# Loading the first chunk of four batches as one group, four tokens to a partition, with the weights in separate tiles

## The chip, the cores and the metric

The kernel runs on one core of one Trainium2 chip. The metric is device time in microseconds (us): the median of repeated runs, each with the granted TensorE clock recorded (the share of full speed that TensorE was allowed, averaged over the run; in the traces of the two kernels it stands at 1.00 or at 0.50). A run counts as slow when it lies over 1.5% above the fastest of the same kernel; all comparisons here use fast runs. The profiled execution gives a span, from the first to the last instruction, which lies about 2 us below the time of the same run (193.5 and 195.28 us before, 201.2 and 203.32 after). Positions ("at 25.1") are microseconds from the start of the span.

Engines are named as the profile names them: PE (TensorE matmul), PEld (its weight loads), DVE (VectorE), ACT (ScalarE), POOL (GpSimd), SP (SyncE); a "q" behind a name is that engine's sequencer, which here mostly means the issuing of DMAs.

## The reference, cut to what matters

```python
batch, n_heads, seq, head_dim = 4, 8, 768, 48       # q, k, v, f_logit, float32
f = 1.0 / (1.0 + np.exp(-f_logit))
for t in range(S):                                   # a gated linear attention
    state = f[:, :, t, :, None] * state + np.einsum('bhd,bhe->bhde', k[:, :, t], v[:, :, t])
    y[:, :, t] = np.einsum('bhd,bhde->bhe', q[:, :, t], state)
x = y.transpose(0, 2, 1, 3).reshape(B * S, H * D)    # 3072 tokens x 384
h = x @ w_in                                         # 384 x 2048
out = (h * sigmoid(h)) @ w_out                       # 2048 x 384
```

The kernel cuts the 768 tokens into six chunks of 128. Within a chunk the recurrence becomes matrix products: sums of log f, keys and queries scaled by exponentials of these sums, masked scores, and a state that is carried from chunk to chunk. A *unit* is one chunk of one batch: units 0 to 3 are chunk 0 of the four batches. The two layers of the feed-forward part take most of TensorE's time. "First layer" below is `x @ w_in`; for chunk 0 it is 192 small matmuls, and nothing of the long, even part of the kernel can start before they are through.

## The kernel before

Every instruction is a task with an engine, a rank and the tiles that it takes and uses. A planner orders the tasks with an estimate of their durations; on the chip each engine then runs its own tasks in exactly that order. So an instruction that waits holds up everything behind it on its engine, needed or not: in the changed kernel GpSimd stood for 10.22 us at one cast, and two key products whose data were there stood behind it.

The loads put one token in each partition. One head of one token is 48 floats, so a piece is 192 bytes:

```python
def load(x, us):                                     # one DMA per tensor and unit, 192 KB
    ...
    nc.sync.dma_start(out=dst, in_=SRC[x].rearrange("b h s d -> s (b h) d")[c * C:(c + 1) * C, b * H:(b + n) * H])
```

Chunk 0 takes 16 such loads, in order of units: f, k, q, v of batch 0, then of batch 1, and so on. Batch 0 can be finished while batch 3 is still loading. v is used as it lands, after a cast on GpSimd (`vb`).

The weights w_in come in two halves and w_out in four pieces, issued by GpSimd as tasks of their own, each released by an earlier task. All halves are slices of one tile:

```python
w_in_sb = sb.tile([128, KT, d_ff], BF16, name="w_in_sb")
w_out_sb = sb.tile([128, NT, d_model], BF16, name="w_out_sb")
...
elif kind == "wi":                                   # half n of w_in
    nc.gpsimd.dma_start(out=w_in_sb[:, :, n:n + w], in_=w_in_src[:, :, n:n + w])
...
for kk in range(KT):                                 # first layer, one unit
    nc.tensor.matmul(h[:, r, :], w_tile(kk, 4 * j + r), at("xT", P)[:, kk, i * C:(i + 1) * C], ...)
```

While TensorE has nothing to do at the start, it runs matmuls on a blank tile ("blank" in the profile; 183 of them, 15.2 us, in the kernel before). They are meant for its clock; no run took them out, so their effect on it is not shown.

## Time and profile before

| what | value | how to read it |
|---|---|---|
| time | 193.28 us, median of 3 runs (192.56 to 193.48) | the metric |
| profiled span | 193.5 us, mean granted clock 0.981 | a run of 195.28 us, with a half clock for 6.8 us |
| PE busy | 179.7 us, 93% | the head holds most of the idle time |
| second half of w_in | issued 25.14, used from 34.16 | the chain of waits; 8.97 us |
| first layer of chunk 0 done | 45.2 us (40.52 + 4.69) | the last piece of that layer in the chain of waits (the work that ended last, followed back) |
| rest of the span | 148.3 us (193.5 - 45.2) | TensorE solid, then a tail of 3.6 us |

The prediction shows the lines. The number to keep is the last one. If the rest does not change, the whole effect of the change is where "first layer of chunk 0 done" moves to.

### The profile page before, as it was taken

The numbers are of one execution on the slowest core, as the hardware profiler recorded it, in microseconds if no ns is written. First come the engines' busy times: TensorE is split into PE (matmuls) and PEld (weight loads), VectorE is DVE, ScalarE is ACT, GpSimd is POOL, SyncE is SP. The second block draws the span as 40 slices with busy tenths as digits, with TensorE's granted clock in tenths as the row PEclk, the third lists the DMA queues.
The fourth block names the chain that finished last, engine by engine and source line by source line (L and its number), as shares of the span: only waits on it lengthen the run. The fifth ranks groups of instructions, "written<-read, shape, count | busy, mean of one in ns | idle before, by whom it ended". The sixth has DMA issues, their size and how long they took to land.

```text
span 193.5 us, 4915 instructions
## 1 busy us (share of the span) xinstructions
PE 179.7 (93%) x2027; PEld 144.8 (75%) x2027; DVE 92.5 (48%) x179; ACT 128.3 (66%) x214; POOL 69.7 (36%) x119
## 2 busy tenths in 40 slices
PE   5976873999999999999999999999999999999992
PEld 4966762997678978778878767878886786877851
DVE  4263556021689447679462776654315455622021
ACT  4425996379229699888897857797597685542700
POOL 2432457001449236173092568331317614200000
PEclk9999998599999999999999999999999999999999
DMA  6999999999999989998328659949994664512112
GB/s 126 202 185 190 223 178 206 205 200 217 205 242 253 232 181 240 194 223 204 72 54 169 152 118 207 200 91 175 184 204 108 152 157 95 136 24 61 41 44 81
DMA packets 119302, 31.12 MB, mean 161 GB/s; under 512 B 116288, under 2 KB 117184, under 8 KB 119280
## 3 DMA queue, kind: packets, MB, share of 16 engines
q1 hardware_dynamic: 116816, 24.32, 64.2%
q0 software_dynamic: 2464, 6.49, 13.8%
q8 instruction: 16, 0.26, 0.5%
q14 instruction: 6, 0.05, 0.1%
HBM read 25.17 MB, written 4.72 MB: 154 GB/s over the span
## 4 chain that ended last, share of the span: by engine, by line
PE 77%; DMA 9%; ACT 6%; SPq 3%; issue 2%; POOL 1%; DVE 0%; DVEq 0%; POOLq 0%
PE mlp L510 31%; PE mlp L500 27%; PE mlp L489 5%; DMA f<-in_f_logit_dram 5%; DMA w_in_sb<-in_moe_w_in_dram 5%; PE sc L553 3%; SPq L455 3%; ACT L631 3%; PE yd L566 2%; PE yd L562 2%; PE tq L542 2%; PE cs L519 2%; PE yd L584 2%; ACT ia L526 1%; PE tq L574 1%
## 5 line engine op out<-in xcount | busy, mean ns | idle before, releaser
L510 PE MATMUL mlp<-w_out_sb,hT 128*128 128x384 bf16 x384 | 69.9, 326 | 0.0
L496 ACT ACTIVATE hT<-mlp 128x512 bf16<-128x512 f32 x80 | 47.1, 597 | 22.4 <-PE mlp L500 19.6
L500 PE MATMUL mlp<-xT,w_in_sb 128*128 128x256 bf16 x480 | 58.3, 273 | 0.3 <-ACT hT L496 0.3
L500 PEld LDWEIGHTS <-w_in_sb 128*128 128x128 bf16 x480 | 51.0, 114 | 2.7 <-issue 0.4
L510 PEld LDWEIGHTS <-hT 128*128 128x128 bf16 x384 | 35.1, 97 | 19.4
L532 POOL TENSOR_TENSOR qk<-k,ia 128x384 bf16<-128x384 f32 x24 | 24.0, 998 | 50.0 <-ACT al L530 38.1
L557 DVE TENSOR_TENSOR atm<-sc,triu 128x512 bf16<-128x512 f32 x48 | 30.9, 685 | 15.4 <-PE sc L553 15.4
L631 ACT ACT_TABLE_LOAD x21 | 26.9, 1283 | 0.4
L595 POOL TENSOR_TENSOR st<-sd,al 48x192 bf16<-48x192 f32 x40 | 20.2, 504 | 13.0 <-DVE sd L589 8.5
L570 DVE CAST yb<-yd 128x384 bf16<-128x384 f32 x24 | 13.3, 555 | 23.7 <-PE yd L566 23.6
L513 DVE COPY o<-mlp 128x384 f32<-128x384 f32 x24 | 13.3, 555 | 22.3 <-PE mlp L510 22.2
L526 ACT ACTIVATE ia<-cs 128x384 f32<-128x384 f32 x24 | 11.7, 488 | 15.5 <-PE cs L523 11.7
L534 POOL CAST vb<-v 128x384 bf16<-128x384 f32 x24 | 11.7, 503 | 20.6 <-DMA v<-in_v_dram 11.1
L489 PE MATMUL mlp<-xT,w_in_sb 128*128 128x128 bf16 x192 | 14.3, 241 | 5.2 <-DMA w_in_sb<-in_moe_w_in_dram 5.0
L536 DVE TENSOR_TENSOR qk<-q,cs 128x384 bf16<-128x384 f32 x24 | 13.2, 549 | 10.0 <-ACT cs L528 9.9
L489 PEld LDWEIGHTS <-w_in_sb 128*128 128x128 bf16 x192 | 13.3, 121 | 5.6 <-DMA w_in_sb<-in_moe_w_in_dram 5.3
L606 PE MATMUL mlp<-blank 128*128 128x128 bf16 x183 | 15.2, 242 | 1.0 <-DVE blank L611 1.0
L462 ACT ACTIVATE e<-f 128x768 f32<-128x768 f32 (+1 forms) x14 | 10.4, 746 | 8.4 <-DMA f<-in_f_logit_dram 8.4
L544 DVE COPY qkT<-tq 128x1024 bf16<-128x1024 bf16 x13 | 8.9, 687 | 13.9 <-PE tq L542 13.9
L606 PEld LDWEIGHTS <-blank 128*128 128x128 bf16 x183 | 12.7, 110 | 1.4 <-DVE blank L611 1.0
L516 POOL DMA_DIRECT2D out_dram<-o x17 | 9.9, 580 | 10.4 <-DVE o L513 7.9
L486 ACT ACTIVATE hT<-mlp 128x512 bf16<-128x512 f32 x16 | 9.3, 597 | 6.0 <-PE mlp L489 5.5
(38 smaller groups left out, 147.1 us busy)
## 6 DMA issues: line engine op xcount, KB each, us to landing
f<-in_f_logit_dram SPq DMA_DIRECT2D x10, 384.0 KB, 6.1
k<-in_k_dram SPq DMA_DIRECT2D x10, 384.0 KB, 5.9
q<-in_q_dram SPq DMA_DIRECT2D x10, 384.0 KB, 5.5
v<-in_v_dram SPq DMA_DIRECT2D x10, 384.0 KB, 6.0
out_dram<-o POOLq DMA_DIRECT2D x17, 192.0 KB, 3.7
w_in_sb<-in_moe_w_in_dram POOLq DMA_DIRECT2D x2, 768.0 KB, 9.0
w_out_sb<-in_moe_w_out_dram POOLq DMA_DIRECT2D x4, 384.0 KB, 9.2
out_dram<-o SPq DMA_DIRECT2D x7, 192.0 KB, 1.9
```

The lines of the kernel that those rows point to most:

```text
L489: nc.tensor.matmul(h[:, r, :], w_tile(kk, 4 * j + r), at("xT", P)[:, kk, i * C:(i + 1) * C], start=(kk == 0), stop=(kk == KT - 1))
L496: return nc.scalar.activation(at("hT", P)[:, 2 * j:2 * j + 2, :], h, AF.Silu)
L500: nc.tensor.matmul(h[:, i, :], w_tile(kk, n), at("xT", P)[:, kk, :], start=(kk == 0), stop=(kk == KT - 1))
L510: nc.tensor.matmul(o, at("hT", P)[:, n, i * C:(i + 1) * C], w_out_sb[:, n, :], start=(n == 0), stop=(n == NT - 1))
L513: nc.vector.tensor_copy(at("ob", u), at("o", u)[:, 0:d_model])
L526: nc.scalar.activation(at("ia", u).rearrange("p h d -> p (h d)"), at("cs", u)[:, 0:HD], AF.Exp)
L532: nc.gpsimd.tensor_mul(at("qk", u)[:, 1, :, 0:D], at("k", P)[:, i], at("ia", u))
L557: nc.vector.tensor_mul(at("atm", u)[:, r], at("sc", u)[:, r], triu[:, None, :].to_broadcast([C, NP, C]))
L570: nc.vector.tensor_copy(at("yb", u), at("y", u))
L595: nc.gpsimd.tensor_mul(at("st", u)[lo:lo + D, :, r * D:(r + 1) * D], at("sd", u)[lo:lo + D, :, r * D:(r + 1) * D], at("al", u)[lo:lo + D, ...
L606: nc.tensor.matmul(buf["mlp", bank][:, 0:C], blank, blank, start=True, stop=True, skip_group_check=True)
L631: nc.scalar.preload_act_table_set(SETS[after[t.idx]])
```

## The change

The intent is to make the loads of chunk 0 cheaper and the vector work on them wider. The four batches' first chunks become one group: partition 32b + n holds tokens 4n to 4n + 3 of batch b. Four tokens of one head lie next to each other in memory, so a piece is 768 bytes instead of 192. The group has its own sums (`within`, `before`), mask (`quads`) and state products. v, which is needed with one token in each partition, is cast in the group's layout and then moved by small DMAs. Separately, the weight pieces get tiles of their own. The planner's ranks are new throughout. Cut to the core:

```diff
-    w_in_sb = sb.tile([128, KT, d_ff], BF16, name="w_in_sb")
-    w_out_sb = sb.tile([128, NT, d_model], BF16, name="w_out_sb")
+    w_in_sb = [sb.tile([128, KT, d_ff // NI], BF16, name=f"w_in{n}") for n in range(NI)]
+    w_out_sb = [sb.tile([128, NT // NO, d_model], BF16, name=f"w_out{n}") for n in range(NO)]
...
+        if kind in ("gf", "gk", "gq", "gv"):         # 8 loads per tensor, 96 KB each: half hh, batch b
+            hh, b = rest
+            src = SRC[kind[1]][b, 4 * hh:4 * hh + 4, 0:C].rearrange("h (n r) d -> n h (r d)", r=4)
+            to = at(kind[1], "g", hh)[32 * b:32 * b + 32]...
+            nc.sync.dma_start(out=to, in_=src)
...
+        elif kind == "gvb":                          # cast v, half hh, all batches
+            nc.gpsimd.tensor_copy(to, split(at("v", "g", hh)))
+        elif kind == "vp":                           # v of one batch to one token in each partition
+            lo = 32 * rest[0]
+            for r in range(4):
+                nc.sync.dma_start(out=at("vb", rest[0])[32 * r:32 * r + 32].rearrange("p h d -> p (h d)"),
+                                  in_=vb_group[lo:lo + 32, r].rearrange("p h d -> p (h d)"))
...
+            if not c:                                # x of chunk 0: tokens back in their order
+                x, t_ps = x.rearrange("p k (n r) -> p k r n", r=4), t_ps.rearrange("p k (r n) -> p k r n", r=4)
+            nc.vector.tensor_copy(x, t_ps)
```

The loads are issued in the order f, k, q of the first four heads, f, k, q of the other four, then all of v. GpSimd's order in the group is: first two key products, issue of w_in's first half, first v cast, last two key products, second v cast, two state updates, issue of w_in's second half.

## The prediction

> **What bounds the kernel now.** I read the page, then the chain of waits in order of time, the head of the timeline, and a table of stretches. From the page:
>
> ```profile
> span 193.5 us, 4915 instructions
> PE 179.7 (93%) x2027; PEld 144.8 (75%) x2027; DVE 92.5 (48%) x179; ACT 128.3 (66%) x214; POOL 69.7 (36%) x119
> ...
> PE   5976873999999999999999999999999999999992
> ...
> PEclk9999998599999999999999999999999999999999
> ```
>
> TensorE (PE) is solid from the eighth slice on and ragged before; the ragged part also holds 183 matmuls on a blank tile[...]. So there is a head of 34 us that waits, and a body that PE fills. The table of stretches (stretch, length, busy time of PE, PEld, DVE, ACT, POOL, granted clock, DMA share, GB/s) says the same:
>
> ```profile
> 25.10:34.20 9.10, 4.91 (x84) 4.00 (x81) 5.04 (x9) 6.90 (x12) 6.49 (x10) 0.91 1.03 188
> 34.20:47.00 12.80, 12.80 (x175) 12.22 (x176) 1.38 (x3) 8.30 (x13) 0.00 (x0) 0.80 1.05 203
> 47.00:70.00 23.00, 23.00 (x264) 17.43 (x262) 16.01 (x30) 14.27 (x26) 11.05 (x19) 1.00 1.06 224
> 70.00:110.00 40.00, 39.69 (x459) 32.15 (x457) 24.77 (x46) 35.00 (x61) 18.07 (x30) 1.00 0.84 173
> ```
>
> What ends the head stands in the chain (start, length, what) and in the timeline (with the idle time before and its releaser):
>
> ```profile
> 25.14 8.97 DMA w_in_sb<-in_moe_w_in_dram
> 34.16 4.03 PE mlp L489 x36
> ...
> 40.52 4.69 PE mlp L489 x84
> ```
>
> ```profile
> 25.14 0.82 POOL L475 DMA_DIRECT2D w_in_sb<-in_moe_w_in_dram  x1 [1.19 <-PE mlp L489]
> ```
>
> Only 48 of the 192 first-layer matmuls of chunk 0 run before the second half of w_in lands at 34.16. GpSimd (POOL) issued it at 25.14, after a wait of 1.19 us for matmuls that read the other half of the same tile. After it the matmuls take 4.03/36 = 112 ns, later 4.69/84 = 56 ns: some 2.5 us go to a half clock. They end at 45.2; the last matmul ends at 189.9 and the span at 193.5. So the end is "end of chunk 0's first layer" + 144.7 us of solid PE + 3.6 us of tail, and the change is read from the head.
>
> [...]after 3.03 us of PE idle the granted clock is 0.50 from 32.6 to 39.4. [...]the loads here are 192 B pieces, and in the first 8 us they arrive at 222 to 225 GB/s[...]. [...]while w_in's first half streams (9.9 to 14.3 us), some 88 packets of 192 B pass per us beside 91 of 2 KB; alone, over 1100 do. The 192 B loads nearly stop.[...]
>
> **The change part by part.** Chunk 0 of the four batches becomes one group: partition = batch and quarter row, four tokens in each, 768 B pieces, in two halves of four heads. The rest of the kernel is the same but for new ranks, one more transposed y by DMA (three PE transposes, 0.17 us, gone) and more stores from POOL.
>
> Loads. 16 loads of 192 KB become 32 of 96 KB on SyncE's queue. An issue with 128 pieces lasts 0.33 us here (the output stores) and 0.05 lies between issues: about 0.38 us each, 96 KB/0.38 = 259 GB/s at best, 12.2 us for all, where the old ones need 3.1 MB/0.22 = 14 us. An issue also waits for the landing of the eighth before it; with some 2.3 us to landing (2.9 for the first 192 KB) that just fits.
>
> Vector work. Exp and log go from 8 of 523 ns to 4 of about 840; the two exps of sums stay 8, the key and query products 4 + 4 at 1.0 and 0.55 us, the transposes 32, their copies 4. The 4 sums of 384 columns and 16 of one become 32 of 192 columns and 16 of four; the 16 state matmuls become 64 with a quarter of the rows. That is PE time in a head with 15.2 us of blank matmuls: free. The v cast stays near 2 us on POOL, and v must then be turned by 16 small SBUF-to-SBUF DMAs, which sit on SyncE's queue.
>
> The chain, walked with these durations: f of the first half lands at 4.2; exp and log to 6.0; sums at half clock, exps, first two key products on POOL to 10.4; w_in's first half issued at 10.4 (before: 6.9), data from 13.4 (3 us, as before). f of the second half waits for ScalarE, whose exps end at 13.9. POOL: v cast, key products 14.8 to 16.8, second v cast. The second v half is issued at 11.4 to 12.5, so part of it meets the w_in stream; with one 768 B packet per weight packet (16/0.21 = 77 per us, 59 KB/us) it lands at about 17.5. Cast to 18.5, state matmuls 1.8, state copies of batches 0 and 1, then their updates on POOL (1.05 each) to 23.2. There w_in's second half is issued: 1.9 us earlier than now. With the same 9.0 us it lands at 32.2.
>
> Scores, outputs and copies run on VectorE from 20.3, one batch per 2.2 us, so x of batch 0 is there at 28 and of the last at 31.5: the 48 matmuls of the first half of w_in fit before 32.2, and with them what the old kernel still did after 34.16 (y of batch 3 and its transposes, 0.5 us).
>
> Sum. First layer ends at 32.2 + 144 x 0.056 = 40.3, against 45.2: 2.0 from the earlier landing, 2.5 from the clock if PE stays awake, 0.5 from y. Then 144.5 + 3.6: 188.4. Against that: the weight stream now runs from about 26 to 37, and q and v of chunk 1, held behind the 16 v DMAs, are issued at 25 and starve until 37; at 220 GB/s they land at 39 to 42, while PE wants them at 40.5 to 44. w_out's last piece is issued only after a key product that needs ScalarE's exp after 16 silus, at about 44.5, and lands near 51.5; PE wants it at 50.5. I put 0.5 to 1 us of PE waits there. About 189.3.
>
> **Rivals.** (a) [...]If issues take 0.45 us[...], the second v half falls fully under the w_in stream, lands near 20 and moves everything after it: w_in at 34.5, end 190.5 to 192. For it: the v loads are last, and POOL takes its work in order.[...] (b) The opposite: issues of 0.33 us put all of v before the w_in stream; state updates end near 20.6, w_in lands at 29.6, end 186. (c) The half clock stays: between 13 and 28 us PE has small bursts and fewer blanks. Then the first layer takes 2.5 us longer: 191 with (a) absent. (d) Starvation after 40 us: q, v or w_out late by 3 us, end 191 to 192. (e) A gain in the body: none, it has no PE idle to give; the lower pace constant alone makes no matmul shorter.
>
> **Range and chances.** (a), (c) and (d) pull up by 1 to 3 us, (b) pulls down by 3; the landing of w_in, good to about 2 us, sets most of it. Range 186.2 to 192.2. The 2% line is 189.4, right at my number: faster 0.53, same 0.44, slower 0.03.
>
> **What would show it.** Right: second half of w_in issued near 23 and landed near 32; granted clock 1.00 from 28 on; first layer's end near 40; 144 us of solid PE after it. Wrong: w_in issued past 25; matmuls of 112 ns after it lands; PE idle between 40 and 55 released by q, v or w_out; or PE solid much earlier than 32, which would mean that the loads beat my 0.38 us.

## The result, and the profile after

The changed kernel is right, and slower: 203.36 us median of 4 runs (202.84 to 204.64), against 193.38 us (192.56 to 196.57) of the kernel before beside it. The ratio is 1.054, with a 95% interval of 1.047 to 1.061. Ratios here are the mean time of one kernel's fast runs over that of the other's in the same rounds, so they are not quite the ratio of the medians that stand beside them. All four runs of the changed kernel are of state fast; of the kernel before, 196.57 is slow.

The page of the profile after, its head:

```profile
span 201.2 us, 5007 instructions
...
PE   6790498589999999999999999999999999999992
...
PEclk9998557879999999999999999999999999999998
```

The digits are tenths of busy time in slices of 5.0 us. The fourth and fifth slice of PE, where it would have worked towards the first layer, are nearly empty (0 and 4), and from the fifth to the ninth slice the clock shows 0.5 to 0.8. From the tenth slice on PE is as solid as before.

The chain of waits tells where the first layer ends (start, length, what):

```profile
13.95 7.63 DMA v<-in_v_dram
...
29.72 1.48 SPq L593
...
33.15 4.99 DMA vb<-vb_group
...
44.44 8.04 PE mlp L636 x144
```

It ends at 44.44 + 8.04 = 52.5, which is 7.3 us later than in the profiled run of before, one of its slower runs. The rest of the span is 201.2 - 52.5 = 148.7 us, against 148.3. So the body is as it was, and the loss lies in the head. The chain names two things: a v load that takes 7.63 us to land, and the moves of v (line 593), of which one takes 4.99 us. Only the moves are new in kind. The chain of the kernel before has a slow load too, an f load of the third batch, under the same stream of w_in's first half:

```profile
7.28 9.25 DMA f<-in_f_logit_dram
```

And the last load of chunk 0 lands at the same time in both kernels, at 22.63 before and at 22.59 after (from the trace's landing events). What differs is how much waits for it: before, one batch; after, the whole group.

The timeline shows how they come about (start, length, engine, instruction, and in brackets the idle time before it and its releaser):

```profile
0.74 1.82 SPq L536 DMA_DIRECT2D f<-in_f_logit_dram  x4
...
10.59 0.93 POOL L622 DMA_DIRECT2D w_in<-in_moe_w_in_dram  x1
...
12.10 8.59 SPq L536 DMA_DIRECT2D v<-in_v_dram  x8
...
20.48 1.02 DVE L561 TENSOR_TENSOR hT<-q,mlp 128x384 bf16<-128x384 f32 x2 [7.18 <-DMA v<-in_v_dram]
...
21.74 0.82 POOL L589 CAST vb_group<-v 128x768 bf16<-128x768 f32 x1 [10.22 <-DMA v<-in_v_dram]
...
25.27 11.01 SPq L593 DMA_DIRECT2D vb<-vb_group  x16
...
30.42 0.82 POOL L622 DMA_DIRECT2D w_in<-in_moe_w_in_dram  x1
...
38.27 0.36 PE L713 MATMUL yd<-vb,atm 128*128 128x48 bf16 x8 [2.06 <-DMA vb<-vb_group]
```

Read it from the top. Four loads take 1.82 us and the next four begin at 2.60, so a load costs (2.60 - 0.74)/4 = 0.47 us of SyncE: 0.43 for the issue, 0.04 between two. The v loads, last in the order, therefore begin at 12.10, when the first half of w_in, issued at 10.59, is about to arrive. In the trace's packet records that stream starts at 12.3 and nearly all of it has started by 18.2. In the full microseconds from 13 to 18 only 24 to 87 packets of 768 B start; from 2 to 12 there were 240 to 307. So the last two q loads land at 17.6 and 20.4 and the v loads between 20.9 and 22.6. The prediction said that an issue also waits for the landing of the eighth DMA before it on SyncE's queue, and here that bites: the last two v loads are issued at 17.60 and 20.38, each 0.02 us after one of those q loads landed, and of SyncE's 8.59 us for the v loads 4.60 are this waiting. (VectorE's wait of 7.18 us for its second q product is put down to v by the profile; it reads q, whose last load landed at 20.36.) GpSimd stands for 10.22 us at the first v cast, and its last two key products, whose data were long there, stand behind it. Then SyncE is busy for 11.01 us with 16 moves of 24 KB each. A move lands 1.8 us after the start of its issue at first, and up to 6.1 us once the second half of w_in streams. The output products of the third batch wait for such a move until 38.27. GpSimd's issue of w_in's second half comes at 30.42, not at 25.14 as before.

The table of stretches (stretch, length, busy time of PE, PEld, DVE, ACT, POOL, granted clock, DMA share, GB/s) has the contrast in two rows:

```profile
2.00:12.00 10.00, 7.72 (x67) 7.35 (x65) 6.11 (x35) 4.74 (x9) 2.86 (x3) 1.00 0.76 203
13.00:20.00 7.00, 2.11 (x42) 1.93 (x39) 0.30 (x1) 1.76 (x5) 0.00 (x0) 0.91 1.06 214
```

In the first row the DMA engines are busy for 0.76 of the time: the loads do not fill them, SyncE's issues set the pace, at 203 GB/s. In the second they are full (a share of 1.06) and every compute engine is nearly idle, GpSimd wholly. From 52.5 on TensorE is solid: 144.22 busy of 144.50 us.

### The profile page after: what moved, and what is told of

It reads as the page before. It is cut to its first block, busy times and chain, and to the rows that moved or that the text cites. A ratio compares the mean times of both kernels' runs of the same rounds, so it can differ in the third digit from the quotient of the medians.

```text
span 201.2 us, 5007 instructions
## 1 busy us (share of the span) xinstructions
PE 182.4 (91%) x2035; PEld 146.6 (73%) x2035; DVE 97.9 (49%) x201; ACT 124.4 (62%) x205; POOL 72.4 (36%) x123
## 4 chain that ended last, share of the span: by engine, by line
PE 72%; SPq 10%; DMA 6%; ACT 4%; issue 3%; POOL 1%; DVE 1%; DVEq 0%; POOLq 0%; ACTq 0%
PE mlp L657 28%; PE mlp L647 25%; SPq L536 6%; PE mlp L636 6%; DMA v<-in_v_dram 4%; SPq L593 4%; PE sc L701 3%; DMA vb<-vb_group 2%; PE yd L713 2%; PE yd L709 2%; PE tq L689 2%; PE cs L666 1%; PE yd L733 1%; ACT L798 1%; ACT hT L643 1%
## 5 line engine op out<-in xcount | busy, mean ns | idle before, releaser
L657 PE MATMUL mlp<-w_out,hT 128*128 128x384 bf16 x384 | 70.2, 326 | 0.0
L647 PE MATMUL mlp<-xT,w_in 128*128 128x256 bf16 x480 | 58.6, 273 | 0.2
L647 PEld LDWEIGHTS <-w_in 128*128 128x128 bf16 x480 | 51.1, 114 | 2.9 <-issue 0.3
L679 POOL TENSOR_TENSOR qk<-k,ia 128x384 bf16<-128x384 f32 x20 | 20.0, 999 | 40.3 <-ACT al L677 29.8
L704 DVE TENSOR_TENSOR atm<-sc,triu 128x512 bf16<-128x512 f32 x40 | 25.7, 684 | 17.5 <-PE sc L701 17.5
L663 POOL DMA_DIRECT2D out_dram<-o x23 | 13.1, 568 | 29.1 <-DVE o L660 28.1
L660 DVE COPY o<-mlp 128x384 f32<-128x384 f32 x24 | 13.2, 555 | 20.9 <-PE mlp L657 20.8
L673 ACT ACTIVATE ia<-cs 128x384 f32<-128x384 f32 x20 | 9.8, 488 | 20.9 <-PE cs L670 16.5
L744 POOL TENSOR_TENSOR st<-sd,al 48x192 bf16<-48x192 f32 x32 | 16.1, 504 | 14.4 <-DVE sd L738 13.1
L681 POOL CAST vb<-v 128x384 bf16<-128x384 f32 x20 | 9.6, 505 | 18.7 <-DMA v<-in_v_dram 18.2
L522 ACT ACTIVATE e<-f 128x768 f32<-128x768 f32 x10 | 8.4, 836 | 9.7 <-DMA f<-in_f_logit_dram 9.7
L636 PE MATMUL mlp<-xT,w_in 128*128 128x128 bf16 x192 | 12.0, 226 | 0.0
L713 PE MATMUL yd<-vb,atm 128*128 128x48 bf16 x192 | 8.8, 184 | 3.5 <-DMA vb<-vb_group 2.1
L636 PEld LDWEIGHTS <-w_in 128*128 128x128 bf16 x192 | 11.6, 116 | 0.0
```

The source lines that it names most:

```text
L647: nc.tensor.matmul(h[:, i, :], w_tile(kk, n), at("xT", P)[:, kk, :], start=(kk == 0), stop=(kk == KT - 1))
L657: nc.tensor.matmul(o, at("hT", P)[:, n, i * C:(i + 1) * C], w_rows(n), start=(n == 0), stop=(n == NT - 1))
L660: nc.vector.tensor_copy(at("ob", u), at("o", u)[:, 0:d_model])
L663: (nc.sync if t.eng == "SP" else nc.gpsimd).dma_start(out=out[r0:r0 + C, :], in_=at("ob", u))
L679: nc.gpsimd.tensor_mul(at("qk", u)[:, 1, :, 0:D], at("k", P)[:, i], at("ia", u))
L704: nc.vector.tensor_mul(at("atm", u)[:, r], at("sc", u)[:, r], (triu if c else quads)[:, None, :].to_broadcast([C, NP, C]))
```

## The experiments

The theory after this reading: two costs of about 4 us each. First, the last q loads and the v loads, issued at 0.47 us each, fall under the stream of w_in's first half, and GpSimd's order carries the delay to all else. Second, the 16 moves of v cost SyncE 11 us and land late under the second half's stream. The rivals: one of the two hides the other; the moves are harmless and only late v matters; the 32-partition loads are slow at the memory itself; or the group's form is slower whatever the loads do.

The table gives the times and the span's split for all runs. "Rest" is the span less the end of chunk 0's first layer; the layer's end is the start of its last piece in the chain plus that piece's length. Medians are of all runs, ratios of the fast ones; every profiled run but that of batch_order (one look, state unknown) is fast. In tiles_w_sooner the chain doesn't pass through the layer's last piece, so its two places are empty. The labels that end in _b repeat an experiment whose edit had a flaw, told below.

| kernel | median us (runs) | ratio to before, 95% | span | first layer ends | rest |
|---|---|---|---|---|---|
| before | 193.38 (192.56 to 196.57) | | 193.5 | 45.2 | 148.3 |
| after | 203.36 (202.84 to 204.64) | 1.054 (1.047 to 1.061) | 201.2 | 52.5 | 148.7 |
| w_after_v | 199.55 (199.23 to 199.97) | 1.041 (1.036 to 1.047) | 197.2 | 48.5 | 148.7 |
| moves_split | 200.85 (200.48 to 201.37) | 1.048 (1.043 to 1.052) | 199.4 | 50.8 | 148.6 |
| moves_split_b | 200.41 (199.65 to 201.76) | 1.037 (1.029 to 1.045) | 197.6 | 48.9 | 148.7 |
| v_from_pool | 199.05 (198.82 to 199.96) | 1.039 (1.034 to 1.044) | 197.5 | 48.8 | 148.7 |
| one_move (wrong result) | 199.31 (198.85 to 199.89) | 1.033 (1.028 to 1.037) | 197.4 | 49.0 | 148.4 |
| w_after_v_one_move (wrong result) | 194.96 (194.47 to 197.0) | 1.012 (1.006 to 1.018) | 192.6 | 44.1 | 148.5 |
| one_move_w_sooner (wrong result) | 195.0 (194.09 to 196.09) | 1.011 (1.004 to 1.018) | 193.6 | 45.2 | 148.4 |
| one_move_w_sooner_b (wrong result) | 194.67 (193.43 to 195.3) | 1.010 (1.007 to 1.013) | 193.1 | 44.7 | 148.4 |
| w_after_v_moves_split | 201.53 (200.13 to 201.78) | 1.043 (1.035 to 1.051) | 199.4 | 50.8 | 148.6 |
| w_after_v_moves_split_b | 201.45 (201.18 to 202.09) | 1.041 (1.035 to 1.046) | 199.2 | 50.6 | 148.6 |
| batch_order | 202.93 (1 run) | | 200.9 | 51.7 | 149.2 |
| tiles_only | 189.67 (189.39 to 192.02) | 0.988 (0.984 to 0.991) | 188.3 | 40.0 | 148.3 |
| tiles_w_sooner | 191.72 (191.1 to 192.32) | 0.994 (0.991 to 0.997) | 189.3 | | |
| tiles_w_sooner_b | 191.02 (190.13 to 191.16) | 0.985 (0.980 to 0.991) | 189.1 | 40.8 | 148.3 |

The last column hardly moves. Whatever an edit did, it did to the head. The kernel before varies more from run to run (191.07 to 194.74 in one set of 19, with granted clocks of 0.982 to 1.000), and its profiled run (195.28 us) is one of the slower ones: beside that set's fastest it would count as slow. Differences among the changed kernels are therefore better read from their own medians and spans than from the ratios.

A flaw of four edits was found only in their traces. The planner places the blank matmuls by the planned start of the task that comes next. A task that I moved *forward* kept its late planned start, and so all blanks up to that start came with it, in one heap in front of useful matmuls: 37 of them, 4.15 us, in moves_split, 10 in the changed kernel at the same place. In the _b runs the moved task takes the start of its new neighbour, and the blanks stay where they were. w_after_v moves a task backward and has no such heap; nor have one_move, w_after_v_one_move, v_from_pool, batch_order and tiles_only.

### w_after_v: the first weight stream behind the v loads

GpSimd issues w_in's first half after the second v cast. Nothing else changes; `behind` moves one task in the planned order.

```diff
     tasks, idles = planned(CFG, SLOTS)
+    behind(("wi", 0), ("gvb", 1))
```

> The changed kernel with one move: GpSimd issues the first half of w_in behind the second v cast instead of before the first one. Theory 1 (starvation: the w_in stream of 13.0 to 18.5 us holds up the last v and q loads, GpSimd waits 10.2 us for v and everything after it slides): the v loads are then bound by their issue alone (32 issues of 0.47 us), the first v cast starts near 16 us instead of 21.7, the second ends near 20 instead of 25.2, the second half of w_in is issued near 25 instead of 30.4, and the first layer ends 4 to 6 us earlier than at 52.5: about 198 us against 203.4. Theory 2 (the cost is SyncE's issue queue: 32 loads and 16 v moves, one after the other): little changes before 18 us and the v moves still take 10 us: 201 to 203. Theory 3 (the head's extra TensorE and VectorE work and its half clock cost the time): no change, 203.

Measured: 199.55 us, 3.8 us less than the changed kernel. The timeline of this run:

```profile
12.10 4.75 SPq L543 DMA_DIRECT2D v<-in_v_dram  x8
...
16.91 0.82 POOL L596 CAST vb_group<-v 128x768 bf16<-128x768 f32 x1 [7.20 <-DMA v<-in_v_dram]
...
20.43 11.78 SPq L600 DMA_DIRECT2D vb<-vb_group  x16
```

The eight v loads start at the same 12.10, but are through in 4.75 us instead of 8.59, and the first cast runs at 16.91 instead of 21.74. So the stream did hold the v loads, by 4.8 us. It held the last q loads as well: VectorE's second q product runs at 14.28 here, against 20.48. So the 3.8 us belong to the last loads together. The moves now begin at 20.43 and meet the delayed first half of w_in: they take 11.78 us of SyncE. The first cost is shown; the second stays.

### moves_split and moves_split_b: the moves from two engines

The moves are issued directly behind the second v cast, and every other one by ScalarE. The second run has the blanks in their old places.

```diff
+    behind(("vp", 0), ("gvb", 1))                    # and vp 1, 2, 3 behind it
...
-                nc.sync.dma_start(out=at("vb", rest[0])[32 * r:32 * r + 32]...
+                (nc.scalar if r % 2 else nc.sync).dma_start(out=at("vb", rest[0])[32 * r:32 * r + 32]...
```

> The changed kernel with the 16 v moves issued half by SyncE and half by ScalarE (idle then), all directly behind the second v cast. Theory 2 (issue queue): the moves take 5 us from 25.3 instead of 11.0, most of them pass before the second w_in stream starts at 32, the last y is not held to 42.0 by a move, and the first layer ends 3 to 5 us earlier: about 199 us. Theory 1 alone (only the v loads matter): the second half of w_in still lands at 39, so at most the part after 39 is saved, under 2 us if the moves were not what held y: 201.5 to 203.

> moves_split repeated without a flaw of its edit: there the tasks moved forward in the order kept their late planned start, and 37 blank matmuls (4.15 us), which are placed by that start, came in one heap before the last transposes of chunk 0 instead of 10 there and 27 later. Here the blanks stay where they are in the changed kernel. If the heap was what ate the gain, TensorE's transposes come at about 25 again and the time falls from 200.85 to 198 to 199. If ScalarE's eight issues are what ate it (its exponential of chunk 1 at 30 again, second half of w_in late), it stays at 200 to 201.

Measured: 200.85 us with the heap of blanks, 200.41 without; a gain of about 3 us, at the lower end of what was expected first, and less than the 198 to 199 that the repetition would have shown if the heap had eaten the gain; it fell in the other branch, 200 to 201, in which ScalarE's eight issues did. The timeline of moves_split_b:

```profile
24.72 7.89 SPq L604 DMA_DIRECT2D vb<-vb_group  x8
24.72 6.00 ACTq L604 DMA_DIRECT2D vb<-vb_group  x8
...
30.76 0.84 ACT L533 ACTIVATE e<-f 128x768 f32<-128x768 f32 x1 [16.05 <-DMA vb<-vb_group]
```

The moves are issued in 7.89 us beside 6.00, where 16 from one engine took 11.01. Of the 16, 13 are issued before w_in's second half, at 29.86. ScalarE pays: its exponential of the next chunk, which ran at 24.80 in the changed kernel, comes at 30.76. The second issuing engine saves some 3 us of issuing (7.89 against 11.01), and the time falls by some 3 us (200.41 against 203.36).

### v_from_pool: the v loads from GpSimd, at the start

```diff
-            nc.sync.dma_start(out=to, in_=src)
+            (nc.gpsimd if kind == "gv" else nc.sync).dma_start(out=to, in_=src)
...
+        early = [t for t in tasks if t.name[0] == "gv"]     # emitted before anything else on GpSimd
```

> The changed kernel with the 8 v loads issued by GpSimd, which is idle from 1.8 to 8.4 us, at its start instead of last on SyncE's queue. Theory 1: v lands before 10 us, GpSimd has no wait of 10 us, the second key products follow ScalarE at 14 to 16, the second v cast ends near 17, the second half of w_in is issued near 22 and lands near 31, the v moves run from 17 to 27, and the first layer ends near 40 to 42: 191 to 194 us. Theory 2: the moves on SyncE still take 10 us but start 8 us earlier, so nearly the same number; it differs from theory 1 only in what holds y. Theory 3: 201 to 203.

Measured: 199.05 us, 4.3 us less than the changed kernel, but 5 us or more above the 191 to 194 expected. The timeline shows who suffers instead:

```profile
11.90 0.83 POOL L589 CAST vb_group<-v 128x768 bf16<-128x768 f32 x1
12.09 1.02 DVE L561 TENSOR_TENSOR hT<-q,mlp 128x384 bf16<-128x384 f32 x2 [5.45 <-DMA q<-in_q_dram]
...
19.80 1.94 POOL L561 TENSOR_TENSOR hT<-k,ia 128x384 bf16<-128x384 f32 x2 [7.07 <-DMA k<-in_k_dram]
```

The first v cast no longer waits, but the loads of k and q do. From 4 to 12 us the DMA engines are now full (a share of 0.98 to 1.12, at 220 to 251 GB/s): with two engines issuing, the DMAs are the bound. The last k and q loads are issued between 9.8 and 14.8 and fall under the stream of w_in, issued at 11.09. So the delay is not v's alone. It goes to whichever loads come last, and all 3.1 MB need 12.5 to 14.3 us at that rate. This corrected the theory: the first cost is "a weight stream started before the last load", not "v too late".

### one_move: four moves instead of sixteen, wrong result on purpose

One DMA of 128 partitions per batch, with the same 96 KB, that puts tokens in the wrong partitions.

```diff
-            lo = 32 * rest[0]
-            for r in range(4):
-                nc.sync.dma_start(out=at("vb", rest[0])[32 * r:32 * r + 32].rearrange("p h d -> p (h d)"),
-                                  in_=vb_group[lo:lo + 32, r].rearrange("p h d -> p (h d)"))
+            nc.sync.dma_start(out=at("vb", rest[0]).rearrange("p h d -> p (h d)"),
+                              in_=vb_group[:, rest[0]].rearrange("p h d -> p (h d)"))
```

> Wrong result on purpose: the changed kernel with 4 moves of v, one of 128 partitions for each batch, in place of 16 of 32 partitions (the rows land in a wrong order; all counts and waits of the other engines stay). If the 16 moves hold the head's end (each issue 0.63 us on SyncE, the last ones caught by the second w_in stream, the last y held to 42.0 us), the moves end near 27.5, the second half of w_in lands at 39 as before, the 144 first-layer matmuls start at 39 to 40 instead of 44.4, and the time falls by 4 to 5 us, to about 199. If they are covered by other waits: 202.5 to 203.5.

Measured: 199.31 us, 4.1 us less than the changed kernel. The same bytes move, from the same tile to the same tiles; only the number of DMAs and the span of partitions of each differ. The timeline has the four moves:

```profile
24.95 2.48 SPq L591 DMA_DIRECT2D vb<-vb_group  x4
```

SyncE spends 2.48 us in place of 11.01, and all moves are issued before w_in's second half, at 30.10. Issue time is per DMA here: 2.48/4 = 0.62 us for 128 partitions, where 32 partitions took 0.59 and 0.04 between two. So four DMAs of 24 KB cost four issues where one of 96 KB costs one, and in this pair of runs the difference is worth 4.1 us of the time.

### w_after_v_one_move: both, wrong result on purpose

Both edits above together.

> Wrong result on purpose: the same 4 moves, and the first half of w_in issued behind the second v cast (w_after_v, 199.6 us). If the two are separate costs that add, the second half of w_in lands near 35 and nothing else holds the first layer: it starts dense at 35 to 36 instead of 40.3, and the time is about 195, still over the 193.2 of before; what then remains is the group's own chain (loads at the same rate as before, one group's sums, state and scores before any first-layer work). If the moves cost nothing here: 199.5.

Measured: 194.96 us, 8.4 us less than the changed kernel. Alone the two gave 3.8 and 4.1, together 7.9. So neither hides the other, and together they carry the kernel from 203.4 to within 1.2% of the kernel before. The chain's last piece of the first layer:

```profile
36.08 8.04 PE mlp L641 x144
```

The layer ends at 44.1, 8.4 us sooner than after. That is also 1.1 sooner than in the profiled run of before, which is one of its slower runs (195.28 us). In time this kernel is still 1.2% slower.

### one_move_w_sooner and one_move_w_sooner_b: the second weight stream earlier still, wrong result on purpose

With both costs gone the group kernel is still not faster than before. These runs ask whether the landing of w_in's second half is what is left. It is issued directly behind the first half; the first run also had a heap of 20 blanks.

```diff
     behind(("wi", 0), ("gvb", 1))
+    behind(("wi", 1), ("wi", 0))
```

> WRONG RESULT ON PURPOSE, as in w_after_v_one_move (195.0 us), from which only the issue of the second half of w_in differs: directly behind that of the first half (20.5 us) instead of behind two state updates (25.75). Question: what makes up the remaining 5.3 us over the before kernel with separate weight tiles (189.7)? Theory 'landing': the second half lands at 34.7 there and sets the start of the 144 dense matmuls at 35.9; with all of w_in landed near 32 the end comes 2 to 3 us sooner, 192 to 193. Rival 'order': VectorE's y copies, scores masks and x copies (busy without a gap from 28.5 to 35.7 us) set that start, and the end moves by less than 1 us; if the earlier stream delays the moves or f of chunk 1, it becomes worse (196).

> WRONG RESULT ON PURPOSE. one_move_w_sooner repeated without its heap of 20 blank matmuls, which held the state products by about 1.4 us. If VectorE's order is the bound of what is left: the start of the dense matmuls as in w_after_v_one_move (36.1) and 194.5 to 195. If the landing of w_in is: 192 to 193.

Measured: 195.0 and 194.67 us, against 194.96 without the edit. In the second run the second half was issued at 21.82 instead of 25.75, and yet the 144 dense matmuls began no earlier:

```profile
20.90 1.71 POOL L629 DMA_DIRECT2D w_in<-in_moe_w_in_dram  x2
...
36.47 8.20 PE L643 MATMUL mlp<-xT,w_in 128*128 128x128 bf16 x144
```

The edit moved the landing far less than the issue. By the trace's landing events the second half landed at 34.48 instead of 35.31, after 12.66 us instead of 9.56, with the first half in flight beside it (both issued from 20.90). It also pushed the landing of the last two moves from 30.0 and 30.2 to 31.5 and 33.2. So these runs test an issue 3.9 us sooner, not a landing 4 us sooner. What they do show is that here the landing does not end last: the dense matmuls begin 2.0 us after it (0.6 us after it without the edit).

What is left can be read in the chain of w_after_v_one_move:

```profile
19.50 1.07 PE mlp L760 x10
...
26.59 1.38 PE mlp L760 x14
...
28.46 0.56 DVE yb L722
```

and in its stretches (columns as above):

```profile
25.00:37.20 12.20, 11.02 (x190) 9.88 (x189) 10.59 (x17) 5.12 (x9) 6.16 (x11) 0.89 1.11 214
```

From 18.9 to 28.5 the chain runs through TensorE: transposes, the group's state products (twice 1.39 us) and, between them, four heaps of blanks (line 760), 3.74 us in all. From 28.5 to 34.2 it runs through VectorE, which is busy for 10.59 of the 12.20 us of the stretch with the masks, casts and x copies of all four batches, one after the other. In the kernel before, three of the four batches had passed through VectorE by 31 us, because batch 0 started on its masks at 10.30. In the group nothing of that can start before the last load. That the order on TensorE and then VectorE's queue are what is left is read from the chain and this row; no edit here shows it, and no run took the blanks out.

### w_after_v_moves_split and w_after_v_moves_split_b: both repairs that keep the result right

```diff
+    behind(("wi", 0), ("gvb", 1))
+    behind(("vp", 0), ("gvb", 1))                    # and vp 1, 2, 3 behind it; every other move from ScalarE
```

> Right result: the changed kernel with both repairs that keep it right: first half of w_in issued behind the second v cast, and the 16 moves of v issued directly behind that cast, half by SyncE and half by ScalarE. Theory 1 (two costs, v held under the weight stream and 16 moves issued one by one): the costs add, but half of the moves' cost stays: 203.4 - 3.8 - 2.5 = about 197. Rival: ScalarE's eight issues again delay its exp and with it GpSimd's second w_in issue, and nothing is gained over w_after_v alone: 199 to 200.

> w_after_v_moves_split repeated without the heap of 37 blank matmuls. If the costs add and half of the moves' cost stays: 197 to 198. If the moves under the first weight stream and ScalarE's issues cancel the gain: 199.5 or more, as w_after_v alone (199.55).

Measured: 201.53 us, and 201.45 without the heap of blanks. The costs do not add here; the two repairs together are 1.9 us worse than w_after_v alone (199.55), and above both branches that the first run expected (197, or 199 to 200). The timeline of the second run:

```profile
20.41 12.66 SPq L605 DMA_DIRECT2D vb<-vb_group  x8
...
28.39 0.84 ACT L534 ACTIVATE e<-f 128x768 f32<-128x768 f32 x1 [13.58 <-DMA vb<-vb_group]
```

Eight moves now take SyncE 12.66 us, longer than sixteen did in w_after_v (11.78) and than eight in moves_split_b (7.89). From moves_split_b this run differs only in the issue of w_in's first half, which comes at 20.33, with the moves: they are in flight while it streams, and one of them takes 7.71 us to land in the chain. ScalarE's exponential is late again (28.39). The two repairs work against each other: delaying the stream puts it on top of the moves.

### batch_order: neighbouring loads on other partitions

The batches are loaded in the order 0, 2, 1, 3, so that consecutive loads write different halves of the 128 partitions.

```diff
-        for b in range(BATCHES):
+        for b in (0, 2, 1, 3):
```

> The changed kernel with the group's loads issued in the batch order 0, 2, 1, 3 instead of 0, 1, 2, 3, so that neighbouring loads write different halves of the partitions.[...] the number of packets in a microsecond stays at 250 to 280 if SyncE's issue of 0.47 us is the bound[...].[...] The time stays within 1 us of 203.4 either way.

Measured in one look: 202.93 us, and about the same rate (195 GB/s from 2 to 12 us, against 203 in the changed kernel). A packet of 768 B took 45 ns in the mean from 2 to 12 us, and 36 ns in the median, in this run as in the changed kernel. From 2 to 11 us, 223 to 282 packets start in a microsecond, against 240 to 307, and the DMA share is 0.79. The order of the batches makes no difference at this rate, at which SyncE's issues set the pace. Whether it would at a higher rate, no run shows.

### tiles_only: the kernel before, with separate weight tiles alone

```diff
-    w_in_sb = sb.tile([128, KT, d_ff], BF16, name="w_in_sb")
+    w_in_sb = [sb.tile([128, KT, d_ff // NI], BF16, name=f"w_in{n}") for n in range(NI)]
...                                                    # likewise w_out, and the two places that read them
```

> The kernel before with one part of the change alone: w_in and w_out in separate tiles, nothing else. If the whole-tile wait of the prediction is real (GpSimd waited 1.19 us for first-layer matmuls before it issued the second half, and first-layer matmuls of the first half were held to its landing), the second half is issued at 24 instead of 25.1, matmuls on the first half go on while it is under way, and the time falls by 1 to 2 us: about 191.5 against 193.2. If these waits were covered by others: no change, within 0.5 us.

Measured: 189.67 us, ratio 0.988 (0.984 to 0.991). It is within 2%, but the whole interval lies below 1: it is faster than both kernels. The chain of waits:

```profile
23.92 7.43 DMA w_in<-in_moe_w_in_dram
31.40 2.20 PE mlp L494 x36
```

GpSimd issues the second half at 23.92 instead of 25.14: the wait of 1.19 us for matmuls that read the other half is gone. It also lands in 7.43 us instead of 8.97; why that is so, no run shows. The data are used from 31.40, 2.8 us sooner, and the 36 matmuls take 2.20/36 = 61 ns each instead of 112: TensorE stood idle for 0.26 us before them and not 3.03, and the granted clock is 1.00. In runs of before with a clock near 1.00 the time is 191.1 to 192.2. So about 2 us of the gain are there without the clock, and the rest goes with it.

### tiles_w_sooner and tiles_w_sooner_b: and the second half sooner still

```diff
+    behind(("wi", 1), ("vb", 2))                      # on top of tiles_only: issued at 19.11, in _b at 18.67
```

> A try for a better kernel: the kernel before with the weights in separate tiles (tiles_only, 189.7 us) and the second half of w_in issued one key product sooner, behind the third v cast (about 19.8 us instead of 23.9; batch 3's loads have then been issued). It lands near 29 instead of 31.3, the first layer starts there, and the time falls by 1 to 2 us to about 188. If the stream catches batch 3's loads, its x comes later than 35.4 and the gain is lost: 189.5 to 191.

> tiles_w_sooner repeated without its heap of 28 blank matmuls. If the loss of 2 us against tiles_only came from the stream that meets the loads of batch 3: 191 to 192 again. If it came from the heap: 189 to 190, or less if the earlier landing pays.

Measured: 191.72 us with a heap of 28 blanks, 191.02 without (runs of the clock 1.00: 190.13 and 190.92, against 189.41 to 190.35 of tiles_only). No gain, and by its own times about a microsecond of loss; the ratios to before (0.985 and 0.988) do not separate the two. So part of the first loss may have been the heap. The timeline of the second run shows why 5 us of earlier issue bring nothing:

```profile
20.25 7.21 SPq L468 DMA_DIRECT2D k<-in_k_dram  x1
```

and its chain has the load that matters:

```profile
19.11 10.00 DMA f<-in_f_logit_dram
```

The stream meets the loads behind it. An issue of chunk 1's k holds SyncE for 7.21 us, and the v cast of batch 3 on GpSimd waits 4.37 us, to 27.79, where tiles_only has it at 24.79. In the chain it is chunk 1's f, which lands after 10.00 us, at 29.1. ScalarE's exponentials of chunk 1 wait for it, and the activations of chunk 0's first layer stand behind them until 33.78. The second half of w_in had landed at 27.49, 3.9 us sooner than in tiles_only, and bought nothing. It is the lesson of v_from_pool once more: a stream that is started before the last load is paid for by that load.

## Why the prediction was wrong

The prediction was 189.3 us in a range of 186.2 to 192.2. The time is 203.36, so even the range failed, and the direction too. The sum has a slip as well: it adds positions in the span and gives the result as the time, which lies about 2 us higher; 189.3 us of span would be some 191 us of time. That is small beside a miss of 14 us.

**What held.** The frame held: the end is "end of chunk 0's first layer" plus a constant. The constant was 148.3 and measured 148.7. There was no gain in the body (rival (e)), and the half to one microsecond of PE waits after 40 us did not come. The first half of w_in was issued at 10.59 (predicted 10.4). The second half of w_in took 7.4 us from issue to landing (predicted 9.0), the first 10.0. The two gains named for the separate tiles and the clock are real, but they belong to the tiles alone: tiles_only has them.

**The step that failed first: "about 0.38 us each, 96 KB/0.38 = 259 GB/s".** I took the 0.33 us of output stores. An issue of these loads measured 0.43 with 0.04 between two. At 96 KB in 0.47 to 0.48 us the new loads run at some 207 GB/s. That is no faster than the old ones: the prediction's 222 to 225 GB/s are their best microseconds, and from 2 to 9 us they average 209. The wider pieces did cost the DMA engines less (36 ns for a packet of 768 B, 15 ns for one of 192 B), but the loads had twice the count and half the size, and SyncE's issues set the pace. No run made the loads fewer. Rival (a) had this number (0.45), and gave it too little weight.

**The step that failed with it: v's first half before the stream, the second "at about 17.5".** The prediction cast the first half of v before 14.8. In the trace both halves lie under the stream, the first is cast at 21.74 and the second at 24.43. Rival (a) saw the second v half land near 20, but put w_in's second half at 34.5 and the end at 192. Issued at 30.42, it landed at 37.8, because GpSimd takes its work in order: the late v also held two key products, both v casts and the updates that stand before the issue of w_in. Its size, with that of the late q loads, was measured by w_after_v: 3.8 us. The estimate of one packet of the loads for each weight packet held only roughly. In the five microseconds from 13 to 18, 264 packets of 768 B start beside 363 of 2 KB, some three for every four, where I had reckoned with one for one (77 a microsecond). In the kernel before, too, the 88 beside 91 are not the whole stream: in the four microseconds from 10 to 14 there are 8 to 95 beside 79 to 93. From issue to landing the v loads took 7.4 us in the median, the new f loads 2.4.

**The term that was missing: the 16 moves of v.** The prediction says that they "sit on SyncE's queue", and uses that only to date the loads of chunk 1. Their own time, from cast to landing, is nowhere in the sum. The outputs of each batch need them. They take 0.63 us of SyncE each, one of them 1.48, 11.0 us in all, and the later ones land after 4 to 6 us under the second weight stream. one_move puts the cost at 4.1 us.

**The clock.** "Granted clock 1.00 from 28 on" failed as a consequence: TensorE stood idle for 6 us before 21.1, and the granted clock was half from 18.7 to 32.3 and again from 39.2 to 42.6. The prediction's reading of the kernel before was loose here: the clock fell at 32.6, only 1.5 us after TensorE's last matmul (31.1), and TensorE had been busy for 1.96 of the 3.6 us before the fall. The fall at 18.7 came after 3.6 us without a matmul (since 15.1); the other one shows that less idleness can be enough.

**What is left without both.** With both costs removed the time is 195.0, still 5.3 us above tiles_only, whose first layer ends 4.1 us sooner (40.0 against 44.1, of runs with clocks of 1.000 and 0.962). The prediction had VectorE pace one batch per 2.2 us with the last x at 31.5. Measured, a batch costs two masks of 0.64, a cast of 0.56 and an x copy of 1.0 us, about 2.85. The 2.2 us leave 0.35 for the copy of x, as before, but it measures 1.00 us: its destination is now spread four tokens apart. (In the same run the copies of later chunks, same shape and not spread, take 0.35 us.) The prediction also called the added TensorE work free; without both costs the state products and the blanks stand in the chain. one_move_w_sooner_b shows that the landing of w_in does not end last; that the orders of TensorE and VectorE are what is left is read from the profile, not shown by an edit.

So the account is: of the 10 us, about 4 come back when the stream no longer holds the last loads, and about 4 when the moves are few; both are shown by runs. The first is no load that lands later than before (22.6 in both kernels) but one that everything waits for, and no run moved the stream in the kernel before. What stays is the group's own order of work, which gives up the early start of batch 0 and takes back what the separate tiles gain; that part is argued.

## What to carry to other kernels

Here the engine that issues the loads set their pace (0.47 us for each of 96 KB, with the DMA engines 0.76 busy), and the number of DMAs counted for more than the width of their pieces (203 GB/s with 768 B, 209 with 192 B). So ask for the issue time of the new form itself before believing a rate, and give every new small DMA its own term in the sum, with the stream that it will meet. Before starting a large weight stream earlier, look at which load is issued last, who waits for it, and what stands behind that waiter in its engine's order. And when a change has two parts that touch different waits, run the cheap one alone: here it was the gain, and the expensive one took it away.
